# Delta-rule attention with a GELU block: weight staging, first-chunk order and unread products

## The chip, the core and the metric

The kernel runs on one core of a Trainium2 chip. The metric is device time in microseconds of one execution: 964.29 us is the median of three runs of the kernel before (963.94 to 965.77). The engines are named as in the profile: PE (matrix products), PEld (its weight loads), DVE (vector), ACT (scalar), POOL and SP. SP computes nothing here, it issues DMAs; ACT has a DMA queue of its own beside its arithmetic.

## What is computed

```python
k_n = k / (np.linalg.norm(k, axis=-1, keepdims=True) + 1e-06)
state = zeros((B, H, D, D))                       # B=4, H=8, S=768, D=48
for t in range(S):
    y[:, :, t] = einsum('bhd,bhde->bhe', q[:, :, t], state)
    v_old = einsum('bhde,bhd->bhe', state, k_n[:, :, t])
    state += bt[..., None] * einsum('bhd,bhe->bhde', k_n[:, :, t], v[:, :, t] - v_old)
x = y.transpose(0, 2, 1, 3).reshape(B * S, H * D) # 3072 tokens of 384
h = x @ w_in                                      # 384 x 2048
g = h * (1.0 / (1.0 + np.exp(-1.702 * h)))
out = g @ w_out                                   # 2048 x 384
```

The two weight matrices come in double precision; everything else is float32.

## The kernel before

The sequence is cut into six chunks of 128 steps. A unit is one chunk of one batch, with its eight heads side by side, so a chunk has four units. Inside a chunk the recurrence is solved as a triangular system: `prepare` transposes k and q of a unit (`psT`, L242), copies the transposes (`kqT`, L243) and forms the Gram products (`psG`, L253), which ACT or DVE copies to `G` (L257 to L261). `G` goes to DRAM (`Nd`, L267), and its 32x32 diagonal blocks come back for all four batches in one tile (`NT`, L273). `invert` turns these blocks into inverses on DVE alone, in one long row of dependent products and sums, and writes them out (`YS`, L347; `Yd`, L350). `assemble` fetches them (`XT`, L365; `XO`, L369) and builds the 128x128 inverse of each head from four short rounds of products (L381, L387, L405, L413) with a copy behind each (L384, L393, L410, L416). `advance` applies it (`psU`, L436), updates the state (`psS`, L448), forms the output (`psY`, L463) and transposes that to `xT` (L482, L483).

Every two units give a `feed_forward` of 256 tokens: `ph` products with `w_in` (L496), the activation to `gT` on ACT (L501), `po` products with `w_out` (L506). `merge` interleaves several such generators in program order by a fixed count of steps, and `take(cost)` draws from `queue`, a list of waiting generators; in the kernel before that queue begins with `weights()`. A scheduler then orders each engine's instructions, except those marked `pinned`.

The weights are 28 parts of raw doubles: 12 of `w_in` (512 KB each) and 16 of `w_out` (384 KB each). `load_weights` fetches a part on ACT's DMA queue into a buffer `raw` of the tag `gT`, which the feed-forward uses later (five buffers), and `from_double` turns it into float32: seven DVE instructions where the part stands alone (`alone`, the first `NA` parts), otherwise five on DVE and one on ACT (L166). `W0 = 7` parts are converted before `prepare` of the first chunk; the others are drawn by `chunk(0, W1)`, nine per unit, so that the feed-forward comes behind them. The opening runs 40 products of zeros (`junk`, L132), whose result nobody reads.

Of the kernel before, what the change touches and what calls it, by code (L numbers as in the profile page):

```python
# [8 lines left out]
F32 = mybir.dt.float32  # L9
I32 = mybir.dt.int32  # L10
# [8 lines left out]
def kernel(  # L19
# [34 lines left out]
    GB = 5  # L54
    W0, W1 = 7, 9.0
    NW, NA = 40, 7
    NS = C * C + C
# [41 lines left out]
    def pinned(op):  # L99

        return lambda *a, **kw: tc.keep_in_program_order(op(*a, **kw))  # L101
# [23 lines left out]
    S_bd = cpool.tile([128, B, NP, 2, D], F32, name="S_bd")  # L125


    junk = wk.tile([128, 512], mybir.dt.bfloat16, tag="G", name="junk", bufs=4)
    nc.vector.memset(junk, 0.0)
    ps_junk = ps_moe.tile([128, 512], F32, tag="moe", name="ps_junk")  # L130
    for _ in range(NW):
        nc.tensor.matmul(ps_junk, lhsT=junk[:, 0:128], rhs=junk, start=True, stop=True)  # L132

# [5 lines left out]

    def from_double(dst, src, n, alone):  # L140

# [31 lines left out]

    def load_weights(part):
        if part < parts_in:
            j, f0 = part % KC, part // KC * N_IN
            dst = w_in[:, j, f0 : f0 + N_IN]
            src = moe_w_in[j * 128 : (j + 1) * 128, f0 : f0 + N_IN]
            n = N_IN
        else:  # L180
            f = part - parts_in
            dst = w_out[:, f, :]
            src = moe_w_out[f * 128 : (f + 1) * 128, :]
            n = DM
        if src.dtype == F32:
            nc.scalar.dma_start(out=dst, in_=src)
        else:
            from_double(dst, src, n, part < NA)

# [43 lines left out]
    def prepare(n):  # L233
# [4 lines left out]
        for i, src in enumerate((kn, qp)):  # L238
            psT = ps_big.tile([128, NP, 128], F32, tag="big", name="psT")
# [8 lines left out]
        for g in range(0, NP, 2):  # L248
# [37 lines left out]
    def invert(c, b0=0, nb=B):  # L286
# [51 lines left out]
        for i in range(0, HS, Q):  # L338
# [16 lines left out]
    def assemble(n):  # L355
# [5 lines left out]
        XO = wk.tile([128, NP, BS], F32, tag="XO", name="XO", bufs=2)  # L361
        Yb = Yd[c][b * H * C : (b + 1) * H * C].rearrange("(h t) i -> t h i", h=H)
        for blk in range(NB):
            r = slice(blk * BS, (blk + 1) * BS)
            nc.sync.dma_start(out=xt[r, :, r], in_=Yb[r])  # L365
        for p, hh in quads:
            qd = 2 * p + hh
            od = slice((2 * p + 1) * BS, (2 * p + 2) * BS)
            nc.sync.dma_start(out=XO[qd * BS : (qd + 1) * BS], in_=Yb[od, hh::2])  # L369
        for p, hh in quads:  # L370
# [12 lines left out]
        P1 = wk.tile([128, NP, BS], F32, tag="P1", name="P1")  # L383
        nc.vector.tensor_copy(P1, ps1)  # L384
        ps2 = ps_big.tile([128, NP, BS], F32, tag="big", name="ps2")
# [23 lines left out]
        P3 = wk.tile([64, H, 64], F32, tag="P3", name="P3", bufs=1)  # L409
        nc.vector.tensor_copy(P3, ps3)  # L410
        ps4 = ps_big.tile([64, H, 64], F32, tag="big", name="ps4")
# [8 lines left out]
    def advance(n, xT):  # L420
# [21 lines left out]
        U = wk.tile([128, H, D], F32, tag="U", name="U")  # L442
        nc.vector.tensor_copy(U, psU)  # L443

# [71 lines left out]

    def weights():
        for part in range(n_parts):
            load_weights(part)
            yield 1.0  # L520

# [20 lines left out]
    def run(work):  # L542
        for _ in work:
            pass

    def chunk(c, share):

        merge((assemble(c * B), 4), (take(share / 2), 4))
        for b in range(B):
# [6 lines left out]
            if c + 1 < NC:  # L556
                works.append((prepare(n + B), 4))
            works.append((take(share), max(1, round(share / 1.3))))
            merge(*works)
# [7 lines left out]

    queue = [weights()]
    for b in range(0, B, HB):
        normalize_first(b)  # L570
    for blk in range(NB):
        nc.scalar.dma_start(out=bI[blk::NB], in_=betas[:, :, blk, :])
    run(take(W0))
    for b in range(B):
        run(prepare(b))
        if b + len(QP) < B:
            load(b + len(QP), ((QP, q),))
    for b in range(B):
# [43 lines left out]
```

## Time and profile before

| | us |
|---|---|
| median of three runs | 964.29 |
| the profiled execution's own time | 958.64 |
| its span | 956.8 |
| start of the first inversion's DVE work | 56.68 |
| first product of the feed-forward | 171 |

| engine | busy us | share of the span |
|---|---|---|
| PE | 870.3 | 91% |
| PEld | 690.8 | 72% |
| DVE | 426.1 | 45% |
| ACT | 213.8 | 22% |
| POOL | 94.6 | 10% |

The shares are averages over stages that differ, so a stage has to be read by itself. "Granted clock" is the share of full speed that the chip gave TensorE in a stretch: 0.50 is 1.2 GHz and 1.00 is 2.4 GHz. In the trace a float32 product of the code stands as two records of PE. What was waited for stands in square brackets behind an arrow.

### The profile page before, as it was taken

How to read it: one execution, taken by the hardware profiler on the slowest of the kernel's cores; microseconds unless marked ns; L12 is line 12 of the kernel's file. 1: busy time of each engine (PE TensorE's matmuls, PEld its weight loads, DVE VectorE, ACT ScalarE, POOL GpSimd, SP SyncE). 2: the span in 40 equal slices, each digit the busy share in tenths (PEclk: the TensorE clock that was granted, in tenths of full speed). 3: DMA queues.
4: the chain of work that ended last, by engine and by line, in shares of the span. 5: the costliest groups of instructions: out<-in, count | busy, mean ns of one | idle time of the engine just before them, and what ended most of it. 6: DMA issues, size and time to landing. Idle time of an engine off the chain costs nothing.

```text
span 956.8 us, 12512 instructions
## 1 busy us (share of the span) xinstructions
PE 870.3 (91%) x5008; PEld 690.8 (72%) x5008; DVE 426.1 (45%) x952; ACT 213.8 (22%) x469; POOL 94.6 (10%) x97
## 2 busy tenths in 40 slices
PE   5600767999999999999999999999999999999998
PEld 2400756886878877878867778868778868789684
DVE  7969867228333238233247233265332274231000
ACT  1400423320222221223211223212223202122010
POOL 3100011220011110011110012200020000000000
PEclk8655555899999999999999999999999999999999
DMA  9922542230232221133311132211221102000000
GB/s 228 246 52 71 151 128 54 46 81 17 47 65 63 56 53 39 29 67 69 68 37 39 33 78 63 53 37 47 42 53 45 48 17 56 17 9 1 8 9 17
DMA packets 173979, 55.98 MB, mean 59 GB/s; under 512 B 141921, under 2 KB 169569, under 8 KB 173921
## 3 DMA queue, kind: packets, MB, share of 16 engines
q1 hardware_dynamic: 165936, 41.90, 20.0%
q10 hardware_dynamic: 7984, 13.27, 4.9%
q8 instruction: 40, 0.66, 0.3%
q14 instruction: 19, 0.15, 0.1%
HBM read 34.70 MB, written 20.45 MB: 58 GB/s over the span
## 4 chain that ended last, share of the span: by engine, by line
PE 86%; DVE 11%; DMA 1%; issue 1%; ACT 1%; ACTq 0%; POOL 0%; SPq 0%; DVEq 0%
PE ph L496 27%; PE po L506 26%; PE psG L253 5%; PE psY L463 5%; PE psU L436 4%; PE ps L405 3%; PE ps L413 3%; PE ps L387 2%; PE ps L381 2%; PE psT L242 2%; PE psS L448 2%; DVE tmp L101 2%; PE psK L428 2%; PE psY L457 2%; DVE P L101 1%; DVE z L101 1%
## 5 line engine op out<-in xcount | busy, mean ns | idle before, releaser
L496 PE MATMUL ph<-xT,w_in 128*128 128x256 f32 x1152 | 273.3, 387 | 0.4 <-DVE o L513 0.4
L506 PE MATMUL po<-w_out,gT 128*128 128x384 f32 x768 | 269.3, 494 | 0.0
L496 PEld LDWEIGHTS ph<-xT,w_in 128*128 128x128 f32 x1152 | 213.5, 192 | 32.8 <-issue 4.6
L506 PEld LDWEIGHTS po<-w_out,gT 128*128 128x128 f32 x768 | 139.1, 190 | 82.7 <-issue 4.0
L501 ACT ACTIVATE gT<-ph 128x512 f32<-128x512 f32 x96 | 57.4, 598 | 249.3 <-PE ph L496 249.0
L253 PE MATMUL psG<-kqT 48*128 48x256 f32 x384 | 63.2, 455 | 12.2 <-ACT kqT L243 12.2
L381 PE MATMUL ps<-XO,L 128*128 128x32 f32 x192 | 27.3, 288 | 46.8 <-DMA XO<-Yd 46.8
L381 PEld LDWEIGHTS ps<-XO,L 128*128 128x128 f32 x192 | 27.8, 215 | 50.0 <-issue 47.5
L198 POOL TENSOR_TENSOR ksq<-KN 128x384 f32<-128x384 f32 x18 | 15.1, 838 | 489.4 <-DMA KN<-in_k_dram 489.4
L463 PEld LDWEIGHTS psY<-U,G 128*128 128x128 f32 x384 | 52.5, 203 | 9.5 <-issue 3.3
L253 PEld LDWEIGHTS psG<-kqT 48*128 48x128 f32 x384 | 39.2, 214 | 26.8 <-ACT kqT L243 14.7
L436 PEld LDWEIGHTS psU<-V,XT 128*128 128x128 f32 x384 | 53.4, 209 | 4.0 <-issue 0.7
L436 PE MATMUL psU<-V,XT 128*128 128x48 f32 x384 | 52.4, 284 | 0.0
L463 PE MATMUL psY<-U,G 128*128 128x48 f32 x384 | 51.5, 281 | 0.0
L257 ACT ACTIVATE G<-psG 128x512 f32<-128x512 f32 x48 | 28.5, 597 | 99.4 <-issue 46.3
L376 DVE STREAM_TRANSPOSE XE<-XT 32x128 f32<-32x128 f32 x96 | 28.9, 301 | 46.8 <-PE ps L387 22.6
L261 DVE COPY G<-psG 128x512 f32<-128x512 f32 x40 | 27.5, 691 | 49.3 <-PE psY L463 38.6
L443 DVE COPY U<-psU 128x384 f32<-128x384 f32 x24 | 13.4, 557 | 78.7 <-PE psU L436 78.7
L375 ACT ACTIVATE L<-G 32x128 f32<-32x128 f32 x96 | 29.5, 307 | 70.2 <-PE ps L381 68.7
L513 DVE COPY o<-po 128x384 f32<-128x384 f32 x24 | 13.2, 549 | 68.5 <-PE po L506 68.5
L387 PE MATMUL ps<-P,XE 128*128 128x32 f32 x192 | 26.4, 284 | 16.6 <-DVE P L384 16.6
L387 PEld LDWEIGHTS ps<-P,XE 128*128 128x128 f32 x192 | 27.2, 209 | 19.7 <-issue 13.4
(92 smaller groups left out, 881.3 us busy)
## 6 DMA issues: line engine op xcount, KB each, us to landing
Nd<-G SPq DMA_DIRECT2D x24, 512.0 KB, 3.2
raw<-in_moe_w_in_dram ACTq DMA_DIRECT2D x12, 512.0 KB, 5.3
raw<-in_moe_w_out_dram ACTq DMA_DIRECT2D x16, 384.0 KB, 3.2
KN<-in_k_dram SPq DMA_DIRECT2D x24, 192.0 KB, 3.2
V<-in_v_dram SPq DMA_DIRECT2D x24, 192.0 KB, 2.8
out_dram<-o SPq DMA_DIRECT2D x24, 192.0 KB, 1.9
QP<-in_q_dram SPq DMA_DIRECT2D x21, 192.0 KB, 3.6
NT<-Nd SPq DMA_DIRECT2D x24, 128.0 KB, 2.6
```

The costliest lines, as they stand in the source:

```text
L101: return lambda *a, **kw: tc.keep_in_program_order(op(*a, **kw))
L253: nc.tensor.matmul(ps[hh][:, i], lhsT=kqT[pr, g + i, 0, :], rhs=kqT[pr, g + i, :, :], start=True, stop=True,)
L375: nc.scalar.activation(l32[o, :, o], G[od, hh::2, 0, ev], ACT.Copy)
L376: nc.vector.transpose(xe[o, :, o], xt[ev, hh::2, ev])
L381: nc.tensor.matmul(ps1[:, g], lhsT=l32[:, g, :], rhs=XO[:, g, :], start=True, stop=True)
L387: nc.tensor.matmul(ps2[:, g], lhsT=xe[:, g, :], rhs=P1[:, g, :], start=True, stop=True)
L405: nc.tensor.matmul(ps3[:, h, :], lhsT=G[hi, h, 0, lo], rhs=xt[hi, h, hi], start=True, stop=True)
L436: nc.tensor.matmul(psU[:, h, :], lhsT=xt[:, h, :], rhs=V[:, h, :], start=True, stop=True)
L463: nc.tensor.matmul(psY[:, h, :], lhsT=G[:, h, 1, :], rhs=U[:, h, :], start=(c == 0 and h == 0), stop=True, skip_group_check=True,)
L496: nc.tensor.matmul(ph[:, u], lhsT=w_in[:, j, f * 128 : (f + 1) * 128], rhs=xT[:, j, :], start=(j == 0), stop=(j == KC - 1),)
L501: nc.scalar.activation(gT[-1][:, f0 % FQ : f0 % FQ + 2], ph, ACT.Gelu_apprx_sigmoid)
L506: nc.tensor.matmul(po, lhsT=gT[f // FQ][:, f % FQ, i * C : (i + 1) * C], rhs=w_out[:, f, :], start=(f == 0), stop=(f == FC - 1),)
```

## The change

Staging and fetching: a raw part no longer has a buffer of its own. The tile `w_out` is still unwritten then, and its bytes hold the raw parts (`stage`): six places for `w_in`, then four, two and one place at its end for `w_out`; the last two parts use a buffer of the tag `xT`. A part is fetched as soon as its place is free (`fetch`, `ahead`), now on SP's queue, and converted later (`convert`). The beta values also go over SP's queue.

Counts: 1 part is converted before the first chunk's `prepare`, 3 behind it, 2 behind the first inversion, and 3, 3, 5, 5 with the four units of chunk 0; the last 6 follow chunk 0. The feed-forward of the first two units is queued ahead of the `w_out` parts.

Order and engines in chunk 0: each unit's transposes are issued ahead of the Gram products of the unit before, and use PSUM buffers of another pool. Units 2 and 3 have half of their `G` copies on DVE. The copies `P1`, `P3` and `U` go to ACT, and so does the issue of the `XO` loads. In all chunks `XO` is issued ahead of `XT`. A small ACT instruction loads the activation table early.

Unread products: 80 at the start in place of 40 of twice the width, 3 behind each unit's transposes, 48 at the end of the first inversion (held back by a `memset` in DVE's order) and 32 with each of the first two units.

```diff
-    W0, W1 = 7, 9.0
-    NW, NA = 40, 7
+    W0, W1, WB = 4, 2, (3, 3, 5, 5)
+    NA = W0
+    NW, NA0, NY, NB0 = 80, 3, 48, 4
...
+    def warm(n, after=None):
+        ps = ps_moe.tile([128, 256], F32, tag="moe", name="ps_warm")
+        if after is not None:
+            after(ps[:, 0:1], 0.0)
+        for _ in range(n):
+            nc.tensor.matmul(ps, lhsT=ones[:, 0:128], rhs=ones, start=True, stop=True)
...
-        raw = wk.tile([128, n, 2], I32, tag="gT", name="raw", bufs=GB)
-        nc.scalar.dma_start(out=raw.bitcast(src.dtype).rearrange("p n o -> p (n o)"), in_=src)
...
+    def stage(part):
+        if part < parts_in:
+            at = part % (FC * DM // (2 * N_IN)) * 2 * N_IN
+            return at, at + 2 * N_IN
+        f = part - parts_in
+        if f >= FC - 2:
+            return None
+        depth = 4 if f < 8 else 2 if f < 12 else 1
+        at = FC * DM - (f % depth + 1) * 2 * DM
+        return at, at + 2 * DM
...
+            if (s := stage(part)) is None:
+                raw = wk.tile([128, DM, 2], I32, tag="xT", name="raw", bufs=3)
+            else:
+                taken[part] = s
+                raw = w_out.rearrange("p f d -> p (f d)")[:, s[0] : s[1]].bitcast(I32)
...
+            nc.sync.dma_start(
+                out=raw.bitcast(src.dtype).rearrange("p n o -> p (n o)"), in_=src
+            )
...
-            if c == 0:
+            if n < HB:
                 nc.scalar.activation(G[:, 2 * g + 1 : 2 * g + 4 : 2], ps[1], ACT.Copy)
...
+        if c == 0:
+            warm(NY, pinned(nc.vector.memset))
         YS = wk.tile([128, BS, BS], F32, tag="P", name="YS")[part]
...
+        eng = nc.scalar if c == 0 else nc.sync
...
+            eng.dma_start(out=XO[qd * BS : (qd + 1) * BS], in_=Yb[od, hh::2])
...
+        copy = nc.scalar.copy if c == 0 else nc.vector.tensor_copy
+        copy(P1, ps1)
...
+            if c == 0:
+                works.append((weights(WB[b]), WB[b]))
+                if b < HB:
+                    works.append((warmth(8, NB0), 8))
...
+    ahead(3)
+    run(weights(1))
+    first = [prepare(b) for b in range(B)]
+    for b in range(B + 1):
+        if b < B:
+            next(first[b])
+            next(first[b])
...
+            warm(NA0)
+        if b > 0:
+            run(first[b - 1])
+            ahead(1)
...
+    run(weights(W0 - 1))
...
     invert(0)
     normalize_first(B)
+    run(weights(W1))
     for c in range(NC):
-        chunk(c, W1 if c == 0 else 9.0 if c + 1 < NC else 15.0)
+        chunk(c, 10.0 if c == 0 else 9.0 if c + 1 < NC else 15.0)
+        if c == 0:
+            run(weights(n_parts))
```

How instructions move on three queues (line numbers of each kernel's own file). First SP's queue around the fourth `Nd` and the fourth `NT`, on which the first inversion waits. Before:

```order
L267 DMA Nd<-G 128x8x128
L86 DMA QP_83<-in_q_dram 128x8x48
L273 DMA NT<-Nd 32x32x32
L267 DMA Nd<-G 128x8x128
L86 DMA QP_81<-in_q_dram 128x8x48
L273 DMA NT<-Nd 32x32x32
L267 DMA Nd<-G 128x8x128
L273 DMA NT<-Nd 32x32x32
L350 DMA Yd<-YS 128x1024
```

Now (the loads into `w_out` are raw parts of `w_in`):

```order
L314 DMA Nd<-G 128x8x128
L97 DMA V<-in_v_dram 128x8x48
L314 DMA Nd<-G 128x8x128
L320 DMA NT<-Nd 32x32x32 x2
L314 DMA Nd<-G 128x8x128
L218 DMA w_out<-in_moe_w_in_dram 128x512 x2
L320 DMA NT<-Nd 32x32x32
L218 DMA w_out<-in_moe_w_in_dram 128x512
L89 DMA QP_81<-in_q_dram 128x8x48
L399 DMA Yd<-YS 128x1024
```

Two raw parts now stand between the fourth `Nd` and the fourth `NT`, and one behind it.

Next DVE in chunk 0 around the second unit. `P_709` and `U` are the copies that PE waits for; L159 to L168 before, and L167 to L176 now, are conversions. Before:

```order
L159 TENSOR_SCALAR tmp<-raw 128x384
L168 SCALAR_TENSOR_TENSOR w_out<-w_out,tmp 128x384
L160 SCALAR_TENSOR_TENSOR w_out<-raw,tmp 128x384
L161 TENSOR_SCALAR tmp<-raw 128x384
L159 TENSOR_SCALAR tmp<-raw 128x384
L161 TENSOR_SCALAR tmp<-raw 128x384
L160 SCALAR_TENSOR_TENSOR w_out<-raw,tmp 128x384
L167 SCALAR_TENSOR_TENSOR tmp<-raw,tmp 128x384 x2
L168 SCALAR_TENSOR_TENSOR w_out<-w_out,tmp 128x384 x2
L384 COPY P_709<-ps_675 128x128
L443 COPY U<-psU 128x384
```

Now:

```order
L426 STREAM_TRANSPOSE XE_88<-XT_85 32x4x32 x2
L168 SCALAR_TENSOR_TENSOR w_in<-w_out,tmp 128x512
L175 SCALAR_TENSOR_TENSOR tmp<-w_out,tmp 128x512
L426 STREAM_TRANSPOSE XE_88<-XT_85 32x4x32 x2
L176 SCALAR_TENSOR_TENSOR w_in<-w_in,tmp 128x512
L169 TENSOR_SCALAR tmp<-w_out 128x512
L450 STREAM_TRANSPOSE XA_89<-XT_85 32x8x32
```

The copies have left DVE, and the parts beside this unit are of `w_in`; no `w_out` part stands on DVE ahead of the second `xT`.

Last PE from the second round of the first unit's end on (`ps_warm` are the unread products). Before:

```order
L413 MATMUL ps_615<-P_613,XA_89 64x64 x8
L381 MATMUL ps_675<-XO,L_87 128x32 x4
L242 MATMUL psT<-ident,KN_79 128x128 x4
L436 MATMUL psU<-V,XT_84 128x48 x8
L387 MATMUL ps_711<-P_709,XE_88 128x32 x4
L242 MATMUL psT<-ident,QP_82 128x128 x4
L448 MATMUL psS<-U,KN_75 128x96 x4
```

Now:

```order
L464 MATMUL ps_682<-P_680,XA_89 64x64 x8
L431 MATMUL ps_720<-XO,L_87 128x32 x4
L289 MATMUL psT<-ident,KN_79 128x128 x4
L487 MATMUL psU<-V,XT_84 128x48 x8
L438 MATMUL ps_755<-P_753,XE_88 128x32 x4
L289 MATMUL psT<-ident,QP_82 128x128 x4
L138 LDWEIGHTS ident
L138 MATMUL ps_warm<-ident 128x256
L499 MATMUL psS<-U,KN_75 128x96 x4
```

The products that are used keep their order. Of chunk 0's 64 unread products 53 stand ahead of the first row shown, and 11 between it and the feed-forward's first product.

## Rows read from the trace of the kernel before

**Rows 1.** Busy time of each engine by stage; the first line names the columns.

```profile
core 0: us, PE busy (x) PEld busy (x) DVE busy (x) ACT busy (x) POOL busy (x), PEclk, DMA share, GB/s
0.00:49.20 49.20, 29.84 (x136) 18.28 (x136) 41.27 (x97) 15.12 (x29) 12.02 (x22) 0.74 1.05 233
56.70:83.20 26.50, 0.00 (x0) 0.00 (x0) 24.95 (x49) 0.66 (x1) 0.00 (x0) 0.50 0.00 0
95.70:171.00 75.30, 56.97 (x299) 51.52 (x299) 56.13 (x136) 26.84 (x60) 9.16 (x8) 0.50 0.42 111
171.00:211.00 40.00, 40.00 (x251) 33.92 (x252) 10.07 (x22) 11.33 (x22) 8.76 (x8) 0.97 0.30 63
249.00:952.00 703.00, 702.61 (x4173) 558.03 (x4172) 253.81 (x553) 152.66 (x346) 63.53 (x58) 1.00 0.19 42
```

**Rows 2.** Timeline of the opening: start, us, engine (q: its queue), line, what, [waited].

```profile
2.24 10.86 PE L132 MATMUL ps_junk<-junk 128*128 128x512 bf16 x40 [2.24 <-DVE junk L129]
...
9.05 10.23 ACTq L149 DMA_DIRECT2D raw<-in_moe_w_in_dram  x5
...
19.19 0.42 DVE L101 TENSOR_SCALAR tmp<-raw 128x512 int32<-128x512 int32 x1
...
22.96 0.42 DVE L101 TENSOR_SCALAR tmp<-raw 128x512 int32<-128x512 int32 x1
...
49.17 0.36 SPq L267 DMA_DIRECT2D Nd<-G  x1
...
54.04 0.32 SPq L273 DMA_DIRECT2D NT<-Nd  x1
56.68 1.23 DVE L101 TENSOR_TENSOR NT<-NT,bI 128x1024 f32<-128x1024 f32 x1 [8.31 <-DMA NT<-Nd]
```

**Rows 3.** DMA alone at 292:294, 240:244.5, 307:310: packets, MB, share of engines.

```profile
q1 hardware_dynamic: 1022, 0.19, 49.1%
q1 hardware_dynamic: 144, 0.52, 29.0%
q1 hardware_dynamic: 1040, 0.52, 62.0%
```

**Rows 4.** PE timeline: first L387 of chunk 0, first L381 of chunk 1.

```profile
95.75 1.88 PE L387 MATMUL ps<-P,XE 128*128 128x32 f32 x8 [1.56 <-DVE P L384]
...
252.20 0.97 PE L381 MATMUL ps<-XO,L 128*128 128x32 f32 x8
```

**Rows 5.** PE by line and shape, 95.7:171: busy us, mean ns, idle before.

```profile
L387 PE MATMUL ps<-P,XE 128*128 128x32 f32 x24 | 5.7, 401 | 16.6 <-DVE P L384 16.6
```

**Rows 6.** Chain of waits: start, us, records of one line, at either clock.

```profile
161.19 1.97 PE ps L413 x16
...
165.16 1.87 PE psU L436 x8
...
185.73 1.07 PE ps L413 x16
...
192.66 0.82 PE psU L436 x8
```

**Rows 7.** Stage table as in rows 1, for stretches around clock changes.

```profile
113.00:135.40 22.40, 22.39 (x115) 20.08 (x115) 15.39 (x36) 8.35 (x19) 1.92 (x2) 0.50 0.51 137
171.00:174.00 3.00, 3.00 (x9) 2.44 (x10) 1.42 (x3) 0.97 (x1) 0.00 (x0) 0.55 0.58 104
849.80:853.20 3.40, 3.01 (x32) 2.54 (x29) 1.24 (x2) 0.49 (x1) 0.00 (x0) 0.96 0.00 0
853.20:856.60 3.40, 3.40 (x13) 2.79 (x11) 0.87 (x2) 0.59 (x1) 0.00 (x0) 0.54 0.00 0
```

**Rows 8.** DVE by line and shape, 95.7:171, conversions: busy us, mean ns.

```profile
L167 DVE SCALAR_TENSOR_TENSOR tmp<-raw,tmp 128x384 int32<-128x384 int32 x16 | 9.6, 611 | 4.0 <-ACT tmp L166 4.0
L160 DVE SCALAR_TENSOR_TENSOR w_out<-raw,tmp 128x384 f32<-128x384 uint32 x16 | 8.8, 548 | 0.0
L159 DVE TENSOR_SCALAR tmp<-raw 128x384 int32<-128x384 int32 x16 | 5.7, 354 | 0.1
```

More of the change, by code (lines that the diff above doesn't have):

```diff
@@ L125 @@
     S_bd = cpool.tile([128, B, NP, 2, D], F32, name="S_bd")
[L128 to L132, printed above, removed]
+    ones = ident.bitcast(mybir.dt.bfloat16)
+    def warm(n, after=None):
[4 more added lines that the diff above has]
+            nc.tensor.matmul(ps, lhsT=ones[:, 0:128], rhs=ones, start=True, stop=True)
+    warm(NW)
+    table = cpool.tile([128, 1], F32, name="table")
+    nc.scalar.activation(table, ident[:, 0:1], ACT.Copy)
     w_in = cpool.tile([128, KC, DFF], F32, name="w_in")
@@ L172, with free, fetch, target @@
     n_parts = parts_in + FC
-    def load_weights(part):
+    stages, taken = {}, {}
+    def stage(part):
[8 more added lines that the diff above has]
+        return at, at + 2 * DM
+    def free(part):
+        s = stage(part)
+        return s is None or all(s[1] <= a or b <= s[0] for a, b in taken.values())
+    def fetch(part):
         if part < parts_in:
             j, f0 = part % KC, part // KC * N_IN
-            dst = w_in[:, j, f0 : f0 + N_IN]
             src = moe_w_in[j * 128 : (j + 1) * 128, f0 : f0 + N_IN]
-            n = N_IN
         else:
             f = part - parts_in
-            dst = w_out[:, f, :]
             src = moe_w_out[f * 128 : (f + 1) * 128, :]
-            n = DM
         if src.dtype == F32:
-            nc.scalar.dma_start(out=dst, in_=src)
+            nc.sync.dma_start(out=target(part), in_=src)
         else:
-            from_double(dst, src, n, part < NA)
+            if (s := stage(part)) is None:
[3 more added lines that the diff above has]
+                raw = w_out.rearrange("p f d -> p (f d)")[:, s[0] : s[1]].bitcast(I32)
+                raw = raw.rearrange("p (n o) -> p n o", o=2)
+            stages[part] = raw
+            nc.sync.dma_start(
+                out=raw.bitcast(src.dtype).rearrange("p n o -> p (n o)"), in_=src
+            )
+    def target(part):
+        if part < parts_in:
+            j, f0 = part % KC, part // KC * N_IN
+            return w_in[:, j, f0 : f0 + N_IN]
+        return w_out[:, part - parts_in, :]
+    def convert(part):
+        if part in stages:
+            dst = target(part)
+            from_double(dst, stages.pop(part), dst.shape[-1], part < NA)
+            taken.pop(part, None)
     ready = {}
@@ L365, in assemble @@
             nc.sync.dma_start(out=xt[r, :, r], in_=Yb[r])
[L366 to L369, printed above, removed]
         for p, hh in quads:
@@ L442, in advance @@
         U = wk.tile([128, H, D], F32, tag="U", name="U")
-        nc.vector.tensor_copy(U, psU)
+        (nc.scalar.copy if c == 0 else nc.vector.tensor_copy)(U, psU)
         if c < NC - 1:
@@ L515, in feed_forward, with ahead, weights, warmth @@
             yield 1.3
[L517 to L520, printed above, removed]
+    order = list(range(n_parts))
+    order[-3], order[-2] = order[-2], order[-3]
+    waiting, staged = order[:], []
+    def ahead(n):
+        while n > 0 and waiting and free(waiting[0]):
+            fetch(waiting[0])
+            staged.append(waiting.pop(0))
+            n -= 1
+    def weights(n):
+        for _ in range(n):
+            if staged:
+                convert(staged.pop(staged.index(min(staged))))
+            ahead(2)
+            yield 0.0
+    def warmth(n, k):
+        for _ in range(n):
+            warm(k)
+            yield 0.0
     def take(cost):
@@ L566, in chunk @@
                 queue.append(feed_forward(c, b - HB + 1, xT))
-    queue = [weights()]
+    queue = []
     for b in range(0, B, HB):
         normalize_first(b)
-    for blk in range(NB):
[L572 to L577, printed above, removed]
+    ahead(3)
[5 more added lines that the diff above has]
+            next(first[b])
+            if b == 0:
+                load(B - 1, ((QP, q),))
+            warm(NA0)
+        if b > 0:
+            run(first[b - 1])
+            ahead(1)
+    for blk in range(NB):
+        nc.sync.dma_start(out=bI[blk::NB], in_=betas[:, :, blk, :])
+    run(weights(W0 - 1))
     for b in range(B):
```

16 lines of the change are left out of this document (11 added, 5 removed).

## The prediction, made before the changed kernel had run

> **What bounds the kernel now.** I read the table by stage first, since the shares of the whole span hide that the stages have different limits [rows 1]. From 249 to 952 us PE is busy 702.61 of 703 us at full clock: nothing that the change does there can be won, and nothing there is changed except the order of two loads. From 171 to 211, the first feed-forward, PE is busy without a gap as well. Everything to be won lies ahead of 171 us, where PE is idle or at half clock (0.50). So the question is when the first feed-forward product starts, and whether the stage behind it still runs without gaps. The work of PE from that product on is the same before and after.
>
> The way to 171 us has three parts. In the opening, until 56.68, DVE waits 8.31 us for the last `NT` load, which was issued at 54.04 behind the last `Nd` at 49.17 [rows 2]. Its cause lies on ACT: it issues weight loads until 9.05 + 10.23 = 19.3 us, so its copies begin late, and DVE converts seven parts beside it. Then comes the inversion on DVE, 56.7 to 83.2, and the way to the first L387 product at 95.75 [rows 1, 4]. Last, from 95.7 to 171, two units are solved with PE busy 56.97 of 75.3 us at half clock, DVE busy 56.13 [rows 1]; 16.6 of PE's 18.3 idle us are three waits at L387 for a copy on DVE [rows 5], which stands there behind conversions.
>
> **The opening.** ACT now issues three loads and can copy from the first transposes on. The Gram copies of all four units should be done by 30 to 35 us, and the three parts that DVE converts behind them (22.96 - 19.19 = 3.8 us each [rows 2]) by 42 to 46. Neither ends last. SP's queue does: it now carries the weights too, and a fetch whose place is still taken holds all that stands behind it. The seventh fetch waits until the first part is read, about 3.1 us after DVE begins it at 19.19 [rows 2], so 22.4. Behind it on SP, up to the fourth `NT`, stand nine loads of 192 KB, two more raw parts, four `Nd` and four `NT`. Alone, a 192 KB load holds the DMA engines 49.1% of 2 us = 0.98 us, 512 KB in one piece 29.0% of 4.5 = 1.31, an `Nd` 62.0% of 3 = 1.86 [rows 3]; for `NT`, with as many packets as a 192 KB load, I take 0.98. That is 9 x 0.98 + 3 x 1.31 + 4 x 1.86 + 4 x 0.98 = 24.1 us, so 46.5 without a gap. The last `NT` lands some 1.7 us behind its own transfer (54.04 to 56.68 is 2.64, less 0.98 [rows 2]), and there are small gaps where `NT` waits for `Nd`: I take 49, a gain of 7.7 us. The lower end is 46; the upper end is the old start less only the three raw parts that no longer stand ahead of it, 56.7 - 3 x 1.31 = 52.8.
>
> In the first 49.2 us the DMA engines are taken to a share of 1.05 over both queues [rows 1]. The Trainium skill, in "DMA: Bandwidth & Descriptors", section "Issuing engines are not separate DMA queues", says that DMAs from all queues run on the same 16 engines and that another issuing engine saves only the time of issue. By that the move between queues frees ACT but no transfer; the inversion would begin at the upper end, and the total be 3.8 us longer.
>
> **Inversion to the first L387.** DVE's row of the inversion gains one `memset`. The two conversions and the normalization behind it are as before, `XO` now goes over ACT, and two fetches wait for conversions between the `XT` loads on SP. The second transposes of `XE` still stand behind the same DVE rows as before, so I count 95.75 - 56.68 = 39.1 us unchanged [rows 2, 4], give or take 2. The 48 unread products fill PE's wait there and cost nothing, since PE has no other work until `XO` lands. L387 then starts at 49 + 39.1 = 88.
>
> **Two units, 75.3 us before.** Here the change takes 16 `w_out` parts out of the stretch. One costs DVE 0.61 + 2 x 0.55 + 2 x 0.35 = 2.4 us (L168 and L161 run like L160 and L159) [rows 8], so 38.5 us go, and three more `w_in` parts of about 3 us come in: DVE falls from 56.1 to about 27 us and no longer sets the pace. The copies `P1`, `P3` and `U` are on ACT, so the 16.6 us of waits at L387 should go. PE's own work depends on the clock. The same records took 1.87 and 0.82 us (L436), and 1.97 and 1.07 (L413) at half and at full clock [rows 6], a ratio of 0.44 to 0.54; with 0.5 the 57.0 us become 28.5. Unread products from here on are 26; 40 of double width took 10.86 us [rows 2], so 0.14 each, 3.6 in all. Idle time left is 18.3 - 16.6 = 1.7, and I add 3 for copies that now stand behind conversions on ACT, which wait for DVE. Sum 37 us at full clock, a gain of 38.3. Ends: 32 (PE without a gap) and 65 (57.0, 26 unread ones at half clock, 1.7).
>
> Whether the clock holds is the largest unknown. For it: products without a pause ran just ahead, and the trace shows the rise after 3 us of `ph` products at 171 to 174 [rows 7]. Against it: from 113 to 135.4 PE was busy 22.39 of 22.4 us with just these small products and stayed at 0.50, and behind 849.8 to 853.2, when PE was busy 3.01 of 3.4 us with such products, it fell from full to half [rows 7]. 53 of the 64 unread products of chunk 0 are issued ahead of the first `psU`, only 11 later. I take a hold as somewhat likelier than any one of the falls, since the Gram products of the next chunk lie between.
>
> The Trainium skill, in "TensorE: Matmul & The Clock Gate", section "What's actually happening", says that the low clock is the default and that activity releases it. By that alone the unread products do what they are there for, and the forecast stands; the row at 849.8 shows a busy PE that lost the clock, and by that row the time is that of the first rival.
>
> If the clock is up when the feed-forward starts, its first 3 us at 0.55 [rows 7] take half: 1.5 us gained.
>
> **The feed-forward stage.** What left the stretch ahead returns here: 16 x 2.4 = 38.5 us of conversions beside DVE's 10.07, in a stage of 40.0 us of PE [rows 1]. 13 parts stand ahead of chunk 0's last copy to `xT` on DVE: 31 + 10 = 41 us against PE's 40, so PE slips by 1 to 3. The rest ends at 49 to 54 us after the stage begins; the first `po` products read `w_out` in order and run beside it. The second inversion can only then begin. Before, it began some 43 us after 171, and its result was wanted by L381 at 252.20 [rows 4], with little to spare. I take 6 us of waits on PE in all, 0 to 12.
>
> **Sum.** The profiled execution took 958.64 us: 958.64 - 7.7 - 38.3 - 1.5 + 6 = 917.1. The median of the runs is 964.29, 5.65 above that execution; the changed kernel should stand the same way: 922.8. The reorder of `XO` and `XT` in later chunks is counted at nothing: PE covers it with feed-forward products, and without that cover a 32 KB load's issue, under 0.5 us a unit, would show.
>
> **Rivals.** *The clock falls on the way.* If it falls once the first unit's inverse is done, nearly all of the rest runs at half: about 60 us in place of 37, so 946; a fall half way gives about 48, so 934. *The unread products do not do what they are for.* Half clock throughout: 65 us and no 1.5, 922.8 + 28 + 1.5 = 952. For both speak the rows just named. *The bound is SP's transfers*, with the upper end of the opening: 927, inside the forecast's range. *Slower.* The `w_out` fetches have four, then two, then one place. If each waited for the conversion ahead of it, a part would cost its transfer, at least 2.6 us from issue to landing as for `NT` [rows 2], and 2.4 of conversion: 16 x 5 = 80 us, and behind the waiting fetch on SP stand the `Nd` and `NT` loads that the second inversion needs, 37 us late. With the clock held that takes the gain to 954; it makes the kernel slower only with the clock at half as well, 952 + 31 = 983, from 18 us of such waits on. Against it: eight parts have four places and can be fetched ahead.
>
> **Chances.** The clock holds: 47%, 912 to 930. It falls half way: 27%, 930 to 943. It falls early or never rises: 17%, 943 to 955. Better than all of that, under 912: 5%. The slower case: 4%. 912 to 944 leaves out about 2 in 10. A difference of 0.2%, 1.9 us, is about what a measurement of this kernel can tell from none: faster 95%, the same 1%, slower 4%.
>
> **What would show it.** Right: DVE starts the inversion near 49; the first L438 (the old L387) near 88; granted clock 1.00 in the 35 us behind it; the first `ph` near 125; PE without long gaps from there but for some microseconds at `po` and at the first product of chunk 1. Wrong: the fourth `NT` landing behind 53; a granted clock of 0.50 between the first `psU` and `ph`; waits of PE for L461 or L494 copies behind conversions on ACT; DVE still converting when PE asks for the last `w_out` parts.

## The result, and the profile after

The changed kernel takes 937.65 us in the median (934.77 to 941.06, four executions), the kernel before 964.12 beside it: a ratio of 0.9737, 95% interval 0.9677 to 0.9797. The profiled execution took 934.82 us, its span 933.1. The forecast was 922.8 us, between 912 and 944: sign and range held, the number was 15 us too low. In the table of the experiments below, executions more than 1.5% above the fastest of their kernel count as slow (two with no unit ahead, four with both edits, three with more unread products); without them these medians are 921.7, 922.4 and 920.1.

| step, in profiled executions, us | before | forecast | changed | changed, second profile |
|---|---|---|---|---|
| inversion starts at | 56.68 | 49 | 54.47 | 52.22 |
| from there to the first L438 (L387 before) | 39.1 | 39.1 | 43.0 | 39.2 |
| from there to the first `ph` | 75.2 | 37 | 39.1 | 38.4 |
| from there to the end of the span | 785.8 | 790.3 | 796.5 | 796.2 |
| span | 956.8 | 915.3 | 933.1 | 926.0 |

The second profile comes from a later measurement (below). 790.3 is 785.8 - 1.5 + 6; 915.3 is the forecast's 917.1 less the 1.8 us by which a time exceeds its span.

The large term came nearly as forecast. Stage table of the changed kernel, columns as in [rows 1], to be set against those rows:

```profile
core 0: us, PE busy (x) PEld busy (x) DVE busy (x) ACT busy (x) POOL busy (x), PEclk, DMA share, GB/s
54.50:97.50 43.00, 15.62 (x94) 12.15 (x94) 37.90 (x89) 3.59 (x8) 0.00 (x0) 0.58 0.19 50
97.50:136.60 39.10, 39.01 (x316) 34.38 (x316) 29.93 (x66) 20.57 (x48) 9.53 (x8) 0.85 0.42 101
...
144.00:216.00 72.00, 66.65 (x346) 50.94 (x345) 60.88 (x136) 21.39 (x42) 9.70 (x8) 1.00 0.42 104
216.00:819.10 603.10, 603.10 (x3667) 480.81 (x3666) 246.52 (x540) 140.04 (x320) 63.58 (x58) 1.00 0.22 49
819.10:832.70 13.60, 13.36 (x70) 11.89 (x70) 3.64 (x9) 2.16 (x6) 0.00 (x0) 0.51 0.00 0
```

Between the first L438 and the first `ph`, PE is busy 39.01 of 39.1 us, where it was busy 56.97 of 75.3; DVE went from 56.13 to 29.93, and the 16.6 us of waits of [rows 5] are gone. The granted clock in that stretch, same columns:

```profile
92.00:98.90 6.90, 6.90 (x36) 5.72 (x36) 3.21 (x9) 1.50 (x5) 0.00 (x0) 0.52 0.45 94
98.90:126.20 27.30, 27.21 (x257) 24.35 (x257) 22.52 (x50) 17.33 (x42) 5.42 (x5) 0.99 0.39 84
126.20:139.80 13.60, 13.60 (x62) 11.15 (x63) 8.79 (x21) 5.11 (x12) 4.11 (x4) 0.51 0.42 127
```

It was full for 27 us and fell 10.4 us ahead of `ph`, with PE busy throughout. What went less well than forecast, 17.8 us of the span, lies elsewhere for the most part.

**The opening, 5.5 us.** The last `NT` load set the start, with PE and the conversions late as well, but not last. PE's timeline (start, us, what, idle before and what ended it), which answers to [rows 2]:

```profile
20.27 2.00 PE L300 MATMUL psG<-kqT 48*128 48x256 f32 x16
22.20 0.66 PE L289 MATMUL psT<-ident,KN 128*128 128x128 f32 x4
29.81 1.09 PE L289 MATMUL psT<-ident,QP 128*128 128x128 f32 x4 [6.95 <-DMA QP<-in_q_dram]
30.69 0.85 PE L138 MATMUL ps_warm<-ident 128*128 128x256 bf16 x3
31.46 5.04 PE L300 MATMUL psG<-kqT 48*128 48x256 f32 x32
```

Unit 3's transposes wait for unit 3's `q`, and behind them stand the Gram products not of one unit but of two (x32): with the order a unit ahead, unit 2's come after unit 3's transposes. That `q` was late because of SP's queue, shown next, where it stands behind the fetch that waited until 23.24 for the conversion of part 0. DVE, shown after it, takes parts 1 to 3 once the Gram copies are out, so from 37.15:

```profile
23.24 0.34 SPq L218 DMA_DIRECT2D w_out<-in_moe_w_in_dram  x1
23.62 0.43 SPq L97 DMA_DIRECT2D V<-in_v_dram  x1
24.16 0.53 SPq L89 DMA_DIRECT2D QP<-in_q_dram  x1
...
39.59 3.11 SPq L320 DMA_DIRECT2D NT<-Nd  x2
42.80 0.51 SPq L314 DMA_DIRECT2D Nd<-G  x1
43.40 1.79 SPq L218 DMA_DIRECT2D w_out<-in_moe_w_in_dram  x2
46.57 0.33 SPq L320 DMA_DIRECT2D NT<-Nd  x1
```

```profile
37.15 0.42 DVE L104 TENSOR_SCALAR tmp<-w_out 128x512 int32<-128x512 int32 x1
...
48.63 0.69 DVE L104 SCALAR_TENSOR_TENSOR w_in<-w_in,tmp 128x512 f32<-128x512 f32 x1
54.47 1.22 DVE L104 TENSOR_TENSOR NT<-NT,bI 128x1024 f32<-128x1024 f32 x1 [5.15 <-DMA QP<-in_q_dram]
```

DVE is done at 49.3 and waits 5.15 us more. The load named in the bracket is not one that this row reads; what it reads is the last `NT`, issued at 46.57 behind two raw fetches. The four `NT` loads took 2.8 us at least, 3.4 in the median and 7.6 at most from issue to landing, and 46.57 + 7.6 is 54.2: the last one was the slow one. PE and the copies didn't hold it: the last Gram copy was out at 37.2, but the fourth `Nd` was issued at 42.80, behind two `NT` issues on SP. From the waiting fetch to that landing the DMA engines were at a mean share of 1.00 (columns as in [rows 1]):

```profile
23.24:54.20 30.96, 6.91 (x40) 5.25 (x41) 15.04 (x26) 4.31 (x8) 3.34 (x3) 0.67 1.00 214
```

In the second profile the last `NT` was issued at 46.92, again behind two raw fetches, and took 5.0 us; DVE waited 1.22 us for it.

**The way to the first L438, 3.9 us.** The timeline of PE and ACT there:

```profile
91.63 1.78 PE L431 MATMUL ps<-XO,L 128*128 128x32 f32 x8 [2.10 <-DMA XO<-Yd]
...
93.22 4.45 PE L138 MATMUL ps_warm<-ident 128*128 128x256 bf16 x20
93.45 0.27 ACT L435 COPY P<-ps 128x128 f32<-128x128 f32 x1 [6.36 <-DMA XT<-Yd]
...
97.47 1.50 PE L438 MATMUL ps<-P,XE 128*128 128x32 f32 x8
```

L438's input `P` was copied by 93.72 and the last `XE` transposed by 93.9; 20 unread products, at half clock, kept PE until 97.5. These are not the 48 behind the inversion, which were over before PE's wait of 2.10 us for `XO`, but part of the 64 of the units.

**Behind the first `ph`, 6.2 us beyond the 4.5 allowed.** PE is idle 5.35 us between 144 and 216 us, which the 0 to 12 allowed for; but it waits at another place than I had said:

```profile
PE psXT L533 <- ACT x L522: 4.1, 2, 2.3
PE ph L547 <- DVE o L564: 1.3, 1, 1.3
```

(waits of PE from 97.5 to 216 us: total, times, longest). Not the second inversion and not `po`. Much later the clock falls for 13.6 us (819.1:832.7 in the stage table), where the profile of before has 3.4 us [rows 7]: some 5 us more, an estimate, half of the difference.

### The profile page after: what moved, and what is told of

Read it like the earlier page. It is cut to its first block, busy times and chain, and to the rows that moved or that the text cites. A ratio compares the mean times of both kernels' runs of the same rounds, so it can differ in the third digit from the quotient of the medians.

```text
span 933.1 us, 12829 instructions
## 1 busy us (share of the span) xinstructions
PE 868.3 (93%) x5172; PEld 691.8 (74%) x5172; DVE 421.2 (45%) x938; ACT 218.6 (23%) x481; POOL 95.9 (10%) x97
## 4 chain that ended last, share of the span: by engine, by line
PE 84%; DVE 10%; DMA 4%; issue 1%; POOL 0%; ACT 0%; SPq 0%; ACTq 0%; DVEq 0%
PE ph L547 26%; PE po L557 25%; PE psG L300 5%; PE psY L514 4%; PE psU L487 4%; PE ps L456 3%; PE ps L464 3%; PE ps L431 2%; PE ps L438 2%; PE psT L289 2%; PE psY L508 2%; PE psS L499 2%; PE psK L479 2%; DVE P L104 1%; DMA QP<-in_q_dram 1%; DMA KN<-in_k_dram 1%
## 5 line engine op out<-in xcount | busy, mean ns | idle before, releaser
L138 PE MATMUL ps_warm<-ident 128*128 128x256 bf16 x204 | 31.8, 321 | 45.4 <-DVE ps_warm L104 43.1
L138 PEld LDWEIGHTS <-ident 128*128 128x128 bf16 x204 | 23.3, 117 | 52.0 <-issue 44.2
L300 PE MATMUL psG<-kqT 48*128 48x256 f32 x384 | 58.5, 417 | 0.0
L487 PEld LDWEIGHTS psU<-V,XT 128*128 128x128 f32 x384 | 49.3, 195 | 3.4
L308 DVE COPY G<-psG 128x512 f32<-128x512 f32 x44 | 30.1, 690 | 45.3 <-PE psY L514 25.2
L487 PE MATMUL psU<-V,XT 128*128 128x48 f32 x384 | 48.1, 270 | 0.0
L300 PEld LDWEIGHTS psG<-kqT 48*128 48x128 f32 x384 | 37.0, 195 | 12.7 <-issue 6.1
L494 DVE COPY U<-psU 128x384 f32<-128x384 f32 x20 | 11.2, 558 | 73.9 <-PE psU L487 73.9
L444 ACT ACTIVATE XT<-ps 32x128 f32<-32x128 f32 x96 | 25.8, 268 | 60.7 <-PE ps L438 59.2
L326 POOL TENSOR_SCALAR_AFFINE_SELECT G<-G 128x1024 f32<-128x1024 f32 x24 | 26.7, 1114 | 119.1 <-DVE G L308 54.6
```

The costliest lines, as they stand in the source:

```text
L138: nc.tensor.matmul(ps, lhsT=ones[:, 0:128], rhs=ones, start=True, stop=True)
L300: nc.tensor.matmul(ps[hh][:, i], lhsT=kqT[pr, g + i, 0, :], rhs=kqT[pr, g + i, :, :], start=True, stop=True,)
L487: nc.tensor.matmul(psU[:, h, :], lhsT=xt[:, h, :], rhs=V[:, h, :], start=True, stop=True)
```

## The experiments

Most are the changed kernel with one edit; the control has none, the last two have more than one, and one starts from the kernel before. The executions of one edited kernel differ by up to 23 us, with the mean granted clock (0.970 at 915.6 us and 0.941 at 938.6 for one of them), so the table has lowest, median and highest of all executions. The kernel before had medians of 962.8 to 963.7 beside them.

| kernel | executions | us | inversion starts | to L438 | to `ph` | clock from L438 to `ph` |
|---|---|---|---|---|---|---|
| changed, again | 6 | 927.8, 938.4, 941.5 | 52.22 | 39.2 | 38.4 | 0.87 |
| no unread products in chunk 0 | 4 | 946.1, 948.7, 949.1 | 52.38 | 38.4 | 63.1 | 0.50 |
| none in the units | 5 | 945.5, 947.0, 949.2 | 52.59 | 39.7 | 60.6 | 0.50 |
| half of those in the units | 6 | 947.0, 949.9, 953.4 | 52.57 | 41.7 | 58.7 | 0.53 |
| before, with unread products | 12 | 956.7, 961.9, 965.4 | 56.80 | 38.8 | 74.7 | 0.58 |
| conversions first | 6 | 955.3, 956.4, 958.3 | 53.42 | 42.2 | 71.8 | 0.62 |
| fetches on ACT's queue | 9 | 950.5, 955.7, 957.8 | 51.36 | 42.7 | 66.1 | 0.50 |
| copies on DVE | 5 | 929.1, 935.3, 937.0 | 52.96 | 40.4 | 42.0 | 0.82 |
| no unit ahead | 6 | 918.5, 922.9, 938.6 | 47.73 | 43.0 | 39.1 | 0.85 |
| unit 3's `q` on ACT's queue | 6 | 923.5, 928.7, 934.8 | 52.33 | 40.3 | 34.8 | 1.00 |
| both of these | 6 | 915.6, 935.2, 938.6 | 49.19 | 43.3 | 47.5 | 0.68 |
| both, more unread products | 6 | 916.9, 928.3, 933.2 | 48.78 | 40.2 | 45.1 | 0.85 |

**The changed kernel again**, as a control.

> The changed kernel once more, as it is, beside the next three. Unit 3's q on ACT's queue gave 923.5 to 934.8 us (median 928.7) against 934.8 to 941.1 of the changed kernel, but its inversion started at 52.33 us, no earlier than in two kernels whose opening is the changed kernel's (52.38 and 52.59). Theory that the moved transfer gave the 9 us: this one stays at 934 to 942 with a median near 938. Rival, the difference is where the clock falls, which varies from execution to execution in the changed kernel too: its runs spread from 924 to 942 here, with a median below 934.

Median 938.4, as in its first measurement (937.65), with one execution at 927.8, the profiled one. The theory's number holds; its reason, the moved `q`, is taken up below.

**No unread products in chunk 0.**

```diff
-        if c == 0:
-            warm(NY, pinned(nc.vector.memset))
...
-                if b < HB:
-                    works.append((warmth(8, NB0), 8))
```

> The changed kernel without the unread products of chunk 0: neither the 48 behind the inversion's last operation nor those between the operations of its first two units (the 80 at the start stay). In the changed kernel's trace the ones from 93.22 to 97.67 us stand between L431 and L438 and hold L438 back by some 3.5 us (its input P was copied by 93.72), and some 4.0 us more of them lie between L438 and the first ph. Theory: they hold the clock. Without them the clock stays at half from about 41 us past the first ph, the 27.3 us at full clock before the first ph (98.9 to 126.2, less 4 us of unread products) become about 46, and 7.5 us of their own time goes: 934.8 + 23 - 7.5 = 950, between 943 and 956. Rival, the clock comes back by itself or the stage isn't bound by it: only their own time goes, 934.8 - 7.5 = 927, between 925 and 933.

948.7 us: the theory. The stage from L438 (L436 here) to `ph`:

```profile
90.70:153.90 63.20, 60.76 (x297) 53.51 (x297) 31.90 (x70) 22.99 (x55) 9.35 (x8) 0.50 0.30 71
```

PE has hardly a gap and takes 63.2 us, because all of it is at half clock; in the changed kernel it is 39.1. On the way to the first L438 this kernel needs 38.4 us, the changed one 43.0 and 39.2. Of these 4.6 and 0.8 us, 3.4 and 0.6 lie between the first L431 and the first L438 (2.47 us here, 5.84 and 3.07 in the changed kernel's two profiles), where the 20 unread products stand.

**None in the units**: only the second of the two edits above.

> The changed kernel with the 48 unread products behind the inversion, but none between the operations of units 0 and 1. Theory that the ones in the units are what holds the clock: full from some 85 us to 92, half from there past the first ph, so about as without any, 934.8 + 23 - 7.5 = 950, 943 to 956. Rival, the 48 suffice, because the units' own products follow close enough (they begin 3.5 us earlier): full clock to the first ph, 934.8 - 7.5 = 927, 925 to 933. Between them (934 to 942): the clock falls half way through the units.

947.0 us, as without any: the 48 behind the inversion raise the clock for 7 us (83 to 90) and it is at half from there to 155.

**Half of those in the units.**

```diff
-    NW, NA0, NY, NB0 = 80, 3, 48, 4
+    NW, NA0, NY, NB0 = 80, 3, 48, 2
```

> The changed kernel with 2 unread products in each group between the operations of units 0 and 1 in place of 4 (32 in place of 64). Theory that all of them are needed: without any the time was 947.0 and the clock fell at 90 us for 65 us; with half, it falls for part of that, and 2 to 4 us of their own time are saved: 938 to 944. Rival, half hold the clock as well, and only their own time counts: 932 to 936 where the changed kernel gives 938.

949.9 us, worse than either number: the clock was at half from 98 to 156 us, as without any. But all 32 ran ahead of the first L438 here (the last ended at 94.4 us), while 26 of the changed kernel's 64 stand behind it, the last at 131.8. So this run doesn't tell their number from their place.

**The kernel before with unread products**: `warm` and `warmth` are added to it and called where the changed kernel calls them.

> The kernel before with one part added: the 48 unread products behind the first inversion and the 64 between the operations of units 0 and 1, at the places that they have in the changed kernel; conversions, queues, opening and copies stay as before. Theory that they hold the clock only where the units' own products follow closely: here P and U still wait for conversions on DVE (16.6 us in the kernel before), the clock falls again within 30 us of the first L387, and the time is 950 to 962. Rival, they hold it by themselves: the 75 us between the first L387 and the first ph become 45 to 55, and the time is 930 to 942.

961.9 us, the theory: no gain. The stage, and PE's waits in it (L404 and L401 are before's L387 and L384):

```profile
95.50:170.20 74.70, 54.40 (x322) 48.35 (x323) 57.62 (x136) 26.91 (x59) 8.72 (x7) 0.58 0.41 112
```

```profile
PE ps L404 <- DVE P L401: 18.6, 2, 12.8
```

The clock was full from 87 to 107 us, but PE stood 18.6 us behind DVE, whose 57.62 us of work are untouched.

**Conversions first**: the 22 remaining parts stand at the head of the queue of fillers, as before.

```diff
+    queue.append(weights(n_parts - W0 - W1, 1.0))
...
-                works.append((weights(WB[b]), WB[b]))
```

> The changed kernel with one part undone: the conversions of the remaining 22 weight parts stand at the head of the queue of fillers, the feed-forward behind them, as in the kernel before; staging, fetches by SP and unread products stay. Theory that this order carries part of the 36 us that were gained between the first L438 and the first ph: the first ph comes one or two units later (145 to 160 us instead of 136.6) with the clock at half by then, and the time is 940 to 955. Rival, the order is worth nothing since the conversions run on DVE, ACT and POOL beside the units either way: 933 to 937. A second rival, that the gain of the conversions' spreading is outweighed by waits in the feed-forward stage (PE idle 5.3 us between 144 and 216): 928 to 933.

956.4 us, slightly beyond the theory's end, with the first `ph` at 167.4. Stage and wait:

```profile
95.60:167.40 71.80, 52.42 (x325) 45.52 (x323) 53.22 (x125) 28.22 (x62) 9.43 (x8) 0.62 0.46 126
```

```profile
PE ps L438 <- DVE XE L426: 17.1, 2, 12.1
```

This is the kernel before over again: DVE back at 53.22 us, PE waiting 17.1 us for DVE (now at `XE`, since `P` is on ACT), and the clock, full until 112, at half from there. Undoing it costs 18 us, about as much as the next edit (17).

**Fetches on ACT's queue.**

```diff
-            nc.sync.dma_start(
+            nc.scalar.dma_start(
                 out=raw.bitcast(src.dtype).rearrange("p n o -> p (n o)"), in_=src
```

> The changed kernel with the raw weight fetches issued by ACT's queue, as in the kernel before, instead of SP's; staging and order stay. Theory that a fetch that waits for a conversion then holds ACT's copies (kqT, Gram, P1, P3, U, XT) as it now holds SP's loads: the inversion starts 1 to 4 us later (the waits of fetches for conversions in the opening), P copies in the units wait 3 to 7 us two or three times: 942 to 955. Rival, SP, which has the loads of q, NT and XT, gains more than ACT loses: 926 to 934.

955.7 us: the theory's sign, not its way. ACT's copies are held in the opening (PE's waits from 15 to 60 us, first fence), yet the inversion starts no later: with no raw fetch on SP, DVE doesn't wait for the last `NT` (second fence). The time goes in the units (third fence), where PE waits for almost nothing:

```profile
PE psT L289 <- ACT kqT L290: 8.5, 1, 8.5
```

```profile
51.36 1.22 DVE L104 TENSOR_TENSOR NT<-NT,bI 128x1024 f32<-128x1024 f32 x1
```

```profile
94.10:160.20 66.10, 65.31 (x315) 56.82 (x315) 29.25 (x67) 23.06 (x56) 9.49 (x8) 0.50 0.27 64
```

The clock fell at 94 and stayed at half with PE busy 65.31 of 66.1 us, unread products among its work until 100.5 and none behind. Why it didn't come back here is open.

**Copies on DVE.**

```diff
-        copy = nc.scalar.copy if c == 0 else nc.vector.tensor_copy
+        copy = nc.vector.tensor_copy
...
-        (nc.scalar.copy if c == 0 else nc.vector.tensor_copy)(U, psU)
+        nc.vector.tensor_copy(U, psU)
```

> The changed kernel with one part undone: in chunk 0 the copies of P1, P3 and U run on DVE again, where the conversions are queued, instead of ACT. Theory that they wait there as in the kernel before (16.6 us in all) and that the clock, which needs dense units, falls with it: the first ph at 150 to 160 us, 945 to 957. Rival, DVE has time for them once the conversions are spread over the units: the copies wait less than 3 us, the clock is as in the changed kernel, 932 to 942.

935.3 us, the rival: PE waits 0.2 us for `P`. With the conversions spread, the engine of these copies doesn't matter.

**No unit ahead** in the opening.

```diff
-    first = [prepare(b) for b in range(B)]
-    for b in range(B + 1):
-        if b < B:
-            next(first[b])
-            next(first[b])
...
-        if b > 0:
-            run(first[b - 1])
+    for b in range(B):
+        run(prepare(b))
```

> The changed kernel without the unit-ahead order in the opening: each unit's two groups of transposes stand directly before its Gram products, so that these wait for ACT's copy of the transposes (0.6 us and the way there and back) with nothing of the next unit between. Theory that this order moved the inversion forward: four such waits of 1 to 1.5 us go back in, and the inversion starts 3 to 6 us later, 938 to 946. Rival, the inversion waits for transfers (q of unit 3, NT of unit 3) and not for PE: it starts within 1 us of 52.4 to 54.5, and the time is that of the changed kernel, 934 to 941.

922.9 us, and neither theory nor rival: the inversion starts 4.5 us *earlier* than in the control. PE, SP and DVE of this kernel:

```profile
24.31 2.00 PE L300 MATMUL psG<-kqT 48*128 48x256 f32 x16 [0.64 <-ACT kqT L290]
29.84 0.64 PE L289 MATMUL psT<-ident,QP 128*128 128x128 f32 x4 [3.53 <-DMA QP<-in_q_dram]
31.17 3.78 PE L300 MATMUL psG<-kqT 48*128 48x256 f32 x16 [0.69 <-ACT kqT L290]
```

```profile
42.54 2.11 SPq L320 DMA_DIRECT2D NT<-Nd  x2
44.74 2.70 SPq L218 DMA_DIRECT2D w_out<-in_moe_w_in_dram  x3
```

```profile
35.64 0.42 DVE L104 TENSOR_SCALAR tmp<-w_out 128x512 int32<-128x512 int32 x1
...
47.73 1.22 DVE L104 TENSOR_TENSOR NT<-NT,bI 128x1024 f32<-128x1024 f32 x1
```

`q` lands as late as ever, but unit 2's Gram products are out of its way (24.31), only unit 3's wait, and the last `NT` loads go out ahead of the raw fetches and take 3.0 to 4.1 us to land. DVE starts without a wait, as soon as its conversions are done. The next run tells which of these counts. This version beats both kernels: four of its six executions lie below the lowest of the changed kernel's ten. 4.5 of the 15.5 us between the medians are the earlier start; the others go with the clock (mean about 0.960 in its two middle executions, 0.946 in the control's), and why it falls less often here is not shown.

**Unit 3's q on ACT's queue.**

```diff
-                load(B - 1, ((QP, q),))
+                load(B - 1, ((QP, q),), nc.scalar)
```

> The changed kernel with one transfer moved: unit 3's q is issued by ACT's queue instead of SP's, where it stands behind the fetch that waited until 23.2 us for the conversion of weight part 0. Theory that this queue position is what held up the opening: that q lands some 3 us earlier, ACT's last kqT comes before 30 us instead of 30.9, Gram copies, Nd and NT move with it, and the inversion starts at 50 to 52 us instead of 54.5: 931 to 933 where the clock falls as in the run of the changed kernel at 934.8. Rival, the raw fetches share the DMA engines with the Nd and NT transfers and set the last NT's landing (7.6 us from issue, three others 2.8 to 3.4): the inversion starts within 1 us of 54.5, and the time stays 934 to 936.

928.7 us, below both ranges and not by the theory. PE no longer waits for that `q`, the last Gram copy is out at 34.9 us (37.2 in the changed kernel) and the conversions are done at 47.0 (49.3), yet the inversion starts at 52.33, as in the control. DVE stands idle for 5.31 us, and what its next row reads is the last `NT`, behind two raw fetches as before. That is the rival's cause:

```profile
42.14 1.77 SPq L218 DMA_DIRECT2D w_out<-in_moe_w_in_dram  x2
45.63 0.33 SPq L320 DMA_DIRECT2D NT<-Nd  x1
```

```profile
52.33 1.23 DVE L104 TENSOR_TENSOR NT<-NT,bI 128x1024 f32<-128x1024 f32 x1 [5.31 <-DMA w_out<-in_moe_w_in_dram]
```

The move has a price as well, from ACT's waits up to 60 us:

```profile
ACT kqT L290 <- DMA bI<-in_beta_dram: 5.9, 1, 5.9
```

The issue of this load, on ACT now, itself waits for an older load and holds ACT's copies 5.9 us. So the time below the control's is not an earlier start. What this profile has is the clock at full all the way:

```profile
92.70:127.40 34.70, 33.66 (x317) 29.75 (x315) 27.83 (x64) 21.21 (x50) 7.88 (x7) 1.00 0.42 96
```

So here the stage of 37 us is seen as it was forecast, with the clock held: 34.7.

**Both of these.**

> The changed kernel with two things at once in the opening: no unit-ahead order (922.9 us alone, inversion from 47.7 us) and unit 3's q on ACT's queue (928.7 alone, inversion from 52.3 us). Theory that both cure the same fault, unit 2's or 3's Gram products standing behind a transpose that waits for that q: together they add little, the Gram products end before 32 us instead of 34.9, the conversions of parts 1 to 3 start by 33, and the inversion starts at 43 to 46 us: 917 to 922. Rival, the conversions or the transfers of NT set the start by then: 46.5 to 48 us, 920 to 925. Second rival, with the conversions earlier their fetches go out before the last NT loads and hold them, as in the run with the q alone: 50 us or later, 924 to 932.

915.6 to 938.6 us with a median of 935.2, beyond all three ranges: two executions lie below 930 and four at 935 or above, too far apart to rank this kernel against either edit alone. The start, 49.19, is the first rival's, 1.2 us late: the last two `NT` go out from 41.76, ahead of the raw fetches at 43.62, and DVE starts without a wait when its conversions are done. The clock in the profile, one of the four long executions:

```profile
93.00:110.00 17.00, 17.00 (x164) 15.09 (x164) 13.11 (x30) 10.32 (x24) 1.22 (x2) 0.99 0.27 50
110.00:144.00 34.00, 34.00 (x161) 29.85 (x161) 18.68 (x42) 12.85 (x30) 8.31 (x7) 0.50 0.35 97
```

**Both, with more unread products** (6 in a group).

> The kernel of the run before with 6 unread products in each group of units 0 and 1 in place of 4 (96 in place of 64). Theory that the clock then holds past the first ph, where it fell for 13 us some 10 us before ph in three of the four traces with 4: 6.5 us gained, 32 more products of 0.11 us on a full PE lost, so 2 to 4 us faster than that run. Rival, they only take PE time: 2 to 4 us slower.

928.3 us, 7 lower in the median, with ranges that overlap nearly wholly: inconclusive. The clock in its profile fell for 14 us (106 to 120) and was back at full before `ph`.

## Why the prediction was right, and where not

*DVE in the units* held: 56.1 to "about 27" was 29.9, and the waits went. The experiments add that the order did this (956.4 us without it); I had credited the copies on ACT too, and they are worth nothing that can be measured.

*The clock in the units* held in the main. 37 us was the sum for a held clock, 34.7 the stage in which it held, 39.1 and 38.4 with a fall ahead of `ph`. The rival "unread products do nothing", at 952, is refuted by the kernel without them, at 948.7. What I had taken for independent is not: the order, the fetches' queue and the unread products each lose 10 to 18 us when undone alone, and unread products alone give nothing. They do not add; in these runs the clock was up for most of the stage only with all three. A rival is left: with half the unread products, with the fetches on ACT, with the conversions first and in the kernel before, the last unread product ended between 94 and 105 us, 58 us or more ahead of `ph`; in the changed kernel the last stands 5 us ahead of it. No run moved them alone, so whether their place or the rest of the edit lost the clock is not shown.

*The opening* is the step that failed, by 5.5 us (3.2 in the second profile), and in it the sum of transfers. That SP's queue ends last was right, the size was not: 24.1 us from 22.4 and a landing 1.7 us later, from prices that each load has alone. The fetch went out at 23.24, and from there to the landing of the last `NT` it was 30.9 us at a DMA share of 1.00. The last `NT` took 7.6 us from issue to landing (5.0 in the second profile) where I had 2.64, because two raw fetches of 512 KB went out just ahead of it. Gram copies and conversions were late too, 37.2 and 49.3 us for my 35 and 46, since I had not followed unit 3's `q`, behind the waiting fetch, to PE, where the unit-ahead order puts two units' Gram products behind it. But that was not the bound: with that `q` moved to ACT's queue both came 2.3 us earlier and the inversion still started at 52.33. Where the last `NT` has no raw fetch ahead of it on its queue (no unit ahead, both edits, fetches on ACT) DVE didn't wait, and the conversions set the start, at 47.73 to 51.36. No run moved that `NT` alone with the unit-ahead order kept.

The Trainium skill, in "DMA: Bandwidth & Descriptors", section "Issuing engines are not separate DMA queues", says that another issuing engine saves only the time of issue. My upper end of 52.8 went with that rule, and 54.47 and 52.22 lie near it. What the rule leaves out is the order on a queue, which the unit-ahead edit changes: 47.73. And which queue issues is worth far more than an issue when an issue waits: 8.5 us of PE's time for a held `kqT` copy with the fetches on ACT, 5.9 of ACT's with one `q`.

*"The 48 unread products cost nothing"* held for the 48, which fit into PE's wait for `XO`. The sum left out that 20 of the units' 64 come between L431 and L438: 3.4 and 0.6 us there, most when they run at half clock. PE had other work by then, which stood behind them in its queue.

*The feed-forward stage*: 6 us of waits were allowed and 5.35 came, at two copies `x` on ACT rather than at `po` and the second inversion. The inversion started 54.8 us after `ph` (191.4 against 136.6), and nobody waited for it. The 1.5 us at `ph` did not come, since the clock was down again there; the fall at 819 us was in no step.

*The slower rival*, fetch and conversion in lockstep, did not show: DVE's waits for a `w_out` fetch from 97.5 to 216 us are

```profile
DVE tmp L167 <- DMA w_out<-in_moe_w_out_dram: 3.7, 2, 3.0
```

*From profile to median* I added 5.65 us; it was 2.83 in the first measurement and 10.7 in the second (927.76 profiled, 938.4 median). This offset goes with the mean granted clock (0.957 in the second profile, 0.945 to 0.948 in the five executions beside it) and differs from one measurement to the next; it belonged in the range alone.

*Signs and luck.* Of the four signs of being wrong two came: the fourth `NT` landed behind 53, and the clock was at half for the 10.4 us ahead of `ph`. The median of 937.65 lies in the band that I had given to a fall half way (930 to 943), not in that of the held clock (912 to 930). But the units were only 2.1 us over their sum; the other steps made up most of the 17.8 us of the span, and the offset to the median gave 2.8 back. So it is luck that this rival's 934 comes so near.

## What to carry to other kernels

When bulk transfers are moved to the queue of the loads on which everything waits, look at what goes out just ahead of the last of these loads, and don't price it with loads that ran alone. Follow also each load that now stands behind a waiting issue to the engine that reads it, and list what stands behind that reader: running a unit ahead puts ready work behind work that is not ready. Then ask which of the two ends last before calling either the cause. Filler products that keep the clock are paid for where real work becomes ready behind them, so they are worth their price only with the waits between the real products gone as well. Parts of one change that serve one end should be tested by undoing each alone and by doing one alone; here neither sum nor difference of the parts gives the whole.

## What the runs showed of the hardware

A busy PE did not bring the clock back by itself. It stayed at half for 63 us with PE busy 60.76 of 63.20 (no unread products), and for 66 us with 65.31 of 66.10 (fetches on ACT), while in the changed kernel it came back after 6.9 us (92.0 to 98.9), 4.45 of them unread products. The Trainium skill, in "TensorE: Matmul & The Clock Gate", section "What's actually happening", says that activity releases the low clock; these rows show stretches in which a busy PE alone did not, and no run here tells what the difference is.

How long the clock is down also differs between executions of one kernel, and the time goes with it: 927.8 us at a mean of 0.957 and 941.5 at 0.947 for the changed kernel.

A wait is not always for what the bracket names: the row of 54.47 us names a load of `q` that it does not read. What it reads, and when that landed, gives the cause.

A load's time to land depends on what goes out just ahead of it: the last `NT` took 7.6 and 5.0 us behind two raw fetches (the changed kernel's two profiles), and 3.0 to 4.1 us was the range of all four `NT` where the last two went out ahead of them (no unit ahead).
